# Choosing experts ahead of a pair's last scores, and an earlier running sum of chunk 1, in a fused gated-attention and mixture-of-experts kernel

## The chip, the cores and the metric

The kernel runs on one core of one Trainium2 chip. The metric is the device time of one execution in microseconds (us), from first to last instruction with what the device needs around them. A profiled execution also has a span: from the program's first instruction to its last.

The engines go by these names: PE is TensorE (matrix products; PEld its weight loads), DVE is VectorE, ACT is ScalarE, POOL is GpSimd, SP is SyncE, which here issues most DMAs. Each engine works through its own instructions in program order and waits on semaphores for the others.

## The reference

Two stages follow one another, in float32. The first is a gated linear recurrence over 4 sequences of 768 steps, with 8 heads of 48 numbers each:

```python
for t in range(S):
    state = alpha[:, :, t, :, None] * state + np.einsum('bhd,bhe->bhde', k[:, :, t], v[:, :, t])
    y[:, :, t] = np.einsum('bhd,bhde->bhe', q[:, :, t], state)
```

Its output becomes 3072 rows of 384 numbers. The second stage routes each row to one of 8 experts and runs that expert alone:

```python
logits = x @ w_gate
expert_idx = np.argmax(logits, axis=1)          # first of equals
h = np.maximum(x_sorted[lo:hi] @ w1[e], 0.0)    # 384 -> 1024, for each expert e
y_sorted[lo:hi] = h @ w2[e]                     # 1024 -> 384
out = gate_w[:, None] * y                       # gate_w: softmax weight of the chosen expert
```

## The kernel before, in words

**Chunks and pairs.** The 3072 rows are 24 chunks of 128 (NT = 24), six to a sequence (NB = 6). For a chunk s the kernel takes the logarithm of alpha (`logs`, L330, ACT), sums it along the chunk with a triangular matrix (`cums`, L341, PE, into the one PSUM tile `cum`), and raises it to exp in both signs (`icp` L344 and `cp` L345, ACT). `operands` (L364, L366, mostly POOL) multiplies k by icp and q by cp into `kqb`. `transposes` (L373, PE) turns both into the PSUM tiles `tp` (two buffers), and ACT and DVE copy them out to kT and qT (L376, L378). `scores` (L386, PE) multiplies them into the PSUM tiles sA and sB; DVE masks sA into dA (L390), ACT copies sB to dB (L392) and POOL masks it (L393). `weighs` (L430) multiplies the masked scores with v into y, `reads` (L418) adds what the state of the chunk before gives. `products` (L452) forms the state's increment in sA for odd chunks and in sB for even ones, so it has to wait until sA or sB was read. For odd chunks DVE adds the old state (accA, L458), and the next scores into sA wait for that; the last chunk of a sequence has no product. `state` (L467, L469, POOL) multiplies by the chunk's decay, which makes a round trip through memory (`decay_out` L350, `decay_in` L355).

**Rows and routing.** `results_to` (L442, DVE) takes y from PSUM. `rows` (L478, PE) turns it to rows and forms minus the logits; DVE sums these to `lgn` (L480). `keep_rows` (L485 ACT, L486 POOL) and `store_rows` (L491, SP) bring the rows to memory. `choose(g)` (L496 to L502, DVE) finds the expert of each row of a group g of chunks as a one-hot matrix `oh`; then POOL adds it to the running counts `ohs`, one addition per chunk (L504). Later `rank_products` (L509, L510, PE) and `slots_of` (L517 to L526, DVE) make a slot of each row, and `one_hots` (L579, L580, DVE), one chunk at a time from the list `hots`, prepares the products that list the tokens by slot (L541, L587). The groups are chunks 0-3, 4-7, 8-11, 12-15, 16-19, 20-21 and 22-23.

**Order.** The order is written out by hand, and the scheduler keeps it on every engine. After a start for chunks 0 to 6 (L629 to L698) comes a loop over pairs, s = 2, 4, ..., 20 (L700 to L779). A turn does reads, weighs and products of chunks s and s + 1, scores of s + 2, running sums and turnings of s + 3 and s + 4, rows of s and s + 1, scores of s + 3, then operands of s + 6, late constants on POOL (`late_consts`), and at its very end, where s + 1 closes a group, `choose` (in turn s = 20, called ORD, for the group 20-21). Loads stand in a list `to_load` and are issued by SP in places, with five buffers each for alpha, k and q. In the start, `keep_busy` (L616) puts products of zeros on PE where it would be idle.

**The experts.** The tail (L805 to L858) finishes chunks 22 and 23, and lists the tokens. Products of the first expert's first layer (`first_layer`, L789) are woven into the tail by `go_ahead(n)`, which issues n matmuls. Blocks of 128 rows are gathered from memory by POOL (L271), turned (`turn_block`, L964, PE), and go through both layers (L972, L988) expert after expert; the result goes out by an indirect DMA (L994). The first expert begins at L1044 with `go_ahead(9)`, ahead of the turning of block 2, the first of the second lot of gathered blocks.

Of the kernel before, what the change touches and what calls it, by code (L numbers as in the profile page):

```python
# [18 lines left out]
def kernel(  # L19
# [71 lines left out]
    ORD = NT - 4  # L91
# [197 lines left out]
    with tc.tile_pool(name="ld", bufs=6) as ld, \  # L289
# [21 lines left out]
        def some_loads(names):  # L311
            for n in names.split():
                load(n[0], int(n[1:]))
# [14 lines left out]
        def logs(s):  # L328
            st[s]["ln"] = work.tile([C, H, D], F32, name="ln")
            nc.scalar.activation(st[s]["ln"][:], st[s]["a"][:], AF.Ln)  # L330
# [7 lines left out]
        def cums(s):  # L338
            d = st[s]
            cum = rps.tile([C, Dm], F32, name="cum")  # L340
            nc.tensor.matmul(cum[:], lhsT=cmask[:], rhs=d["ln"][:], start=True, stop=True)  # L341
            d["icp"] = work.tile([C, Dm], F32, name="icp")
            d["cp"] = cpb[(s + 1) // 2 % len(cpb)][:, (s + 1) % 2, :, :D]
            nc.scalar.activation(d["icp"][:], cum[:], AF.Exp, scale=-1.0)  # L344
            nc.scalar.activation(d["cp"], heads(cum), AF.Exp)  # L345
# [22 lines left out]
        def transposes(s):  # L368
            d = st[s]
            for i, n in enumerate(("kT", "qT")):  # L370
                tp = ps.tile([C, NP, C], F32, name="tp", bufs=2)
                for p in range(NP):
                    nc.tensor.transpose(tp[:, p, :], pair(kqb[s % 4][:, i], p), ident[:])  # L373
                d[n] = work.tile([C, NP, C], F32, name=n, bufs=2 + i)
                if i:
                    nc.vector.tensor_copy(d[n][:], tp[:])  # L376
                else:
                    nc.scalar.copy(d[n][:], tp[:])  # L378
# [114 lines left out]
        def choose(g):  # L493

            t, n = slice(g[0], g[-1] + 1), len(g)
            nc.vector.tensor_reduce(lmin[:, t], lgn[:, t, :], axis=AX, op=ALU.min)  # L496
            sc = work.tile([C, n, E], F32, name="sc")
            nc.vector.tensor_tensor(sc[:], lgn[:, t, :], lmin[:, t].unsqueeze(2).to_broadcast([C, n, E]), op=ALU.is_le)
            nc.vector.tensor_tensor(sc[:], sc[:], first_w[:, None, :].to_broadcast([C, n, E]), op=ALU.mult)
            top = work.tile([C, n], F32, name="top")  # L500
            nc.vector.reduce_max(top[:], sc[:], axis=AX)
            nc.vector.tensor_tensor(oh[:, t, :], sc[:], top[:].unsqueeze(2).to_broadcast([C, n, E]), op=ALU.is_equal)  # L502
            for s in g:
                nc.gpsimd.tensor_add(ohs[:, s + 1, :], ohs[:, s, :], oh[:, s, :])  # L504

# [25 lines left out]
        def close_early(pos):  # L531

            cnt = work.tile([1, 1], F32, name="cnt")
            nc.vector.tensor_scalar(cnt[:], pos, scalar1=float(EC), scalar2=-1.0, op0=ALU.min, op1=ALU.mult)
            nc.vector.scalar_tensor_tensor(
                ohs[0:1, TE, 0:1], in0=cnt[:], scalar=float(EC), in1=ohs[0:1, TE, 0:1], op0=ALU.add, op1=ALU.add,
            )
# [69 lines left out]
        def do(f, i, *a):  # L607
            if 0 <= i < NT:
                f(i, *a)
# [16 lines left out]
        nc.scalar.preload_act_table_set("natural_log_exp_and_others")  # L626
        hots = []

        some_loads("a0 k0 q0 a1 k1 q1")  # L629
        first_consts()  # L630
        keep_busy(5)
        back_consts()
        for i in range(4):
            late_consts(i)
        logs(0)
        cums(0)
        keep_busy(3)
        operands(0, nc.vector, nc.vector)
        some_loads("a2 v0")
        decay_out(0, nc.scalar)  # L640
        logs(1)
        transposes(0)
        cums(1)
        operands(1)
        decay_in(0, nc.scalar)
        scores(0)
# [53 lines left out]
        for s in range(2, NT - 2, 2):  # L700
            more_loads(2)
            if s == 2:
                store_rows(0)
            do(decay_out, s + 4)
            more_loads(2)

            for _ in range(8 if s > NT - 8 else 0):
                next(parts, None)
            y = results_of(s)
            reads(s)  # L710
            reads(s + 1)

            weighs(s, 0)
            weighs(s, 1)
            products(s + 1)
            products(s + 2)
            weighs(s + 1, 0)
            results_to(s, y, 0)
            weighs(s + 1, 1)
            results_to(s, y, 1)  # L720
            state(s + 1)
            do(logs, s + 5)
            if hots:
                one_hots(hots.pop(0))
            scores(s + 2)
            do(logs, s + 6)
            do(cums, s + 5)
            ranks = y[0][:].rearrange("r i p t -> r (i p t)")
            ranked = [rank_products(g, ranks[:, : len(g) * E]) for g in groups_of if g[-1] == s - 1]
            counts = ranks[:, C : C + E]  # L730
            if s in (TE, ORD):

                nc.tensor.matmul(
                    counts, lhsT=ones_sq[:], rhs=ohs[:, s, :], start=True, stop=True, skip_group_check=True,
                )
            if s == ORD:
                early_slots(ranks[:, 2 * C : 2 * C + EB * NQ])
                fetch_lot(0)
            for r in ranked if s < ORD else ():
                slots_of(*r)  # L740
            transposes(s + 3)
            do(operands, s + 5)
            state(s + 2)
            rows(s)
            keep_rows(s)
            store_rows(s - 1)
            if s == ORD:
                for r in ranked:
                    slots_of(*r)
                key = standing(counts[0:1, :])  # L750
                one_hots(hots.pop(0))
                one_hots(hots.pop(0))
                route = rps.tile([C, Dm], F32, name="cum")
                tokens_of_slots(0, TE)
            do(cums, s + 6)
            do(transposes, s + 4)
            more_loads(5)
            do(decay_in, s + 4)
            rows(s + 1)
            keep_rows(s + 1)  # L760
            if s == TE:
                close_early(counts[0:1, 0:1])
            scores(s + 3)
            do(operands, s + 6)
            store_rows(s)
            if s == 2:

                nc.sync.dma_start(x_d[N // 2 : N // 2 + 1, :], zero_w[:])
            late_consts(s + 2)
            late_consts(s + 3)  # L770
            if s == ORD:
                choose(groups_of[-2])
            if hots:
                one_hots(hots.pop(0))
            for g in groups_of[:-2]:
                if g[-1] == s + 1:
                    choose(g)
            for _ in range(4 if s == NT - 8 else 0):
                next(parts, None)  # L779
        for _ in parts:  # L780
# [51 lines left out]
        keep_rows(s + 1)  # L832
        store_rows(s + 1)
        choose(groups_of[-1])
        tokens_of_slots(TE, NT - 4)
        go_ahead(3)

# [204 lines left out]

    for i in range(E):
        if i == 0:  # L1044
            go_ahead(9)
            for k in range(EB, needed[0][-1] + 1):
                turn_block(k)
                go_ahead(3)
            go_ahead(99)
            layer1(w_t[0][0], xT[0], h_t[0], EC, cols[0])  # L1050
        else:
            if i == E - 1:

                nc.gpsimd.drain()
            h_t[i] = (wk if i % 2 else early).tile([C, FB, CAP], F32, name="h_sb", bufs=1)
            if cols[i] < caps[i]:
                nc.gpsimd.memset(h_t[i][:, :, cols[i] : caps[i]], 0.0)
            layer1(w_t[i][0], xT[i], h_t[i], 0, cols[i])

        coming = list(needed[i + 1]) if i + 1 < E else []  # L1060
        for k in coming[:2]:
            turn_block(k)
        if i == 0:
            for n in (1, 2):
                weights1(n, True)
                weights2(n)
            gates_lot(0)
            gates_lot(1)
            for n in range(3, E):
                slots(n)  # L1070
            rows_out(o_idx[:], g_idx[:])
        if i + 3 < E:
            weights1(i + 3)
        for n, k in enumerate(ended[i]):
            if k not in gw:
                gates_lot([k in lot for lot in lots].index(True))
            results(k)
            if n == 0:
                for j in coming[2:]:
                    turn_block(j)  # L1080
                if i and i + 2 < E:

                    weights2(i + 2)
        if i in (0, 1, 3):
            fetch_lot((2, 3, None, 4)[i])
        if i == 0:
            nc.vector.tensor_copy(tot[:], route[0:1, NC : NC + E])
            extra_blocks()
# [48 lines left out]
```

## Time and profile before

| what | value |
|---|---|
| median of 10 runs | 431.08 us (429.81 to 432.19) |
| profiled execution, its own time | 431.05 us |
| its span | 429.3 us, granted TensorE clock 0.997 |
| busy in the span: PE / DVE / ACT / POOL | 419.6 / 142.4 / 108.1 / 141.4 us |
| moved by DMA | 59.43 MB |

By stage (view of windows: us of the window, then the busy time of each engine):

| stage | window | PE | DVE | ACT | POOL | DMA share |
|---|---|---|---|---|---|---|
| start, to the first scores | 0 to 10.20 | 8.72 | 6.71 | 3.93 | 4.33 | 0.85 |
| on to the middle of turn s = 4 | 10.20 to 49.06 | 37.77 | 19.07 | 21.49 | 25.56 | 0.94 |
| rest of the loop | 49.06 to 140.17 | 89.61 | 61.33 | 45.03 | 60.17 | 0.91 |
| tail | 140.17 to 158.85 | 18.02 | 12.67 | 5.47 | 6.96 | 0.30 |
| experts | 158.85 to 429.30 | 265.47 | 42.60 | 32.17 | 44.38 | 0.33 |

How to read the profile's lines. A timeline line has the start in us from the span's start, the duration in us, the engine, the line of the kernel, the operation, tile written <- tiles read, the shape, a count, and in brackets the engine's idle time before it with what ended it. A line of waits names who waited, for whom, the sum in us, how many times, and the longest. Matmuls overlap: the next group's first one usually starts a little before the last one of the group before has drained.

### The profile page before, as it was taken

Reading aid. Unit: us, or ns where it says so; the run is one execution under the profiler, and the core shown is the slowest. Engines: PE = TensorE matmul, PEld = TensorE weight load, DVE = VectorE, ACT = ScalarE, POOL = GpSimd, SP = SyncE. Lnnn points to the kernel's source line nnn. Section 1 sums busy time; section 2 is a strip of 40 time slices with the busy share of each in tenths; the row PEclk is TensorE's granted clock in tenths of the full one; section 3 lists DMA queues with packets and bytes.
Section 4 is the critical chain, followed back from the end, with each engine's and each line's share of the span. In section 5 each row is a group of like instructions: output and inputs, shape, how many; then the busy total and the mean of one; then the engine's idle time right before and its main releaser. Section 6 shows DMA issues by size and latency. Waiting matters only on the chain.

```text
span 429.3 us, 7702 instructions
## 1 busy us (share of the span) xinstructions
PE 419.6 (98%) x2990; PEld 284.7 (66%) x2990; DVE 142.4 (33%) x414; ACT 108.1 (25%) x230; POOL 141.4 (33%) x256
## 2 busy tenths in 40 slices
PE   8999999999999999999999999999999999999995
PEld 6888788888889888655555556655655455555452
DVE  6435657585858843721012101201201101111100
ACT  4465554555442321110111111011110111011011
POOL 4486677576665250160160120024010010011011
PEclk9999999999999999999999999999999999999998
DMA  8999999999977242995541710624530050000000
GB/s 166 170 167 205 198 202 188 202 194 196 185 205 206 95 104 75 397 398 177 192 113 51 274 37 14 259 83 116 214 117 18 2 183 20 0 33 20 1 33 30
DMA packets 132576, 59.43 MB, mean 138 GB/s; under 512 B 114614, under 2 KB 127452, under 8 KB 132538
## 3 DMA queue, kind: packets, MB, share of 16 engines
q1 hardware_dynamic: 127720, 48.96, 44.1%
q0 software_dynamic: 3328, 9.94, 7.1%
q8 instruction: 24, 0.39, 0.4%
q10 hardware_dynamic: 1490, 0.02, 0.2%
q14 instruction: 14, 0.11, 0.1%
HBM read 49.32 MB, written 9.98 MB: 138 GB/s over the span
## 4 chain that ended last, share of the span: by engine, by line
PE 60%; issue 28%; POOL 4%; DVE 4%; DMA 2%; ACT 1%; POOLq 0%; DVEq 0%; ACTq 0%; SPq 0%
PE zp L988 16%; PE hp L972 14%; PE sA L386 5%; PE xr L478 4%; PE tp L373 4%; PE y L430 4%; PE cum L341 3%; POOL out_dram L994 3%; PE y L418 2%; PE xr L616 2%; PE xtp L964 1%; POOL xg L271 1%; PE sB L452 1%; PE hp L789 1%; DMA a_sb<-in_alpha_dram 1%
## 5 line engine op out<-in xcount | busy, mean ns | idle before, releaser
L988 PE MATMUL zp<-w,h_sb 128*128 128x384 f32 (+2 forms) x560 | 137.1, 487 | 0.0
L972 PE MATMUL hp<-xT,w 128*128 128x416 f32 (+5 forms) x384 | 123.9, 483 | 0.0
L988 PEld LDWEIGHTS zp<-w,h_sb 128*128 128x128 f32 (+2 forms) x560 | 73.6, 163 | 56.3 <-issue 14.8
L972 PEld LDWEIGHTS hp<-xT,w 128*128 128x128 f32 x384 | 71.8, 190 | 50.7 <-issue 30.5
L994 POOL DMA_INDIRECT out_dram<-zo,o_idx x26 | 25.8, 992 | 213.3 <-ACT zo L993 208.4
L977 DVE TENSOR_SCALAR h_sb<-hp 128x416 f32<-128x416 f32 (+5 forms) x32 | 17.7, 554 | 148.1 <-PE hp L972 148.1
L993 ACT ACTIVATE zo<-zp,gw 128x384 f32<-128x384 f32 x26 | 15.1, 581 | 123.7 <-PE zp L988 119.1
L979 ACT ACTIVATE h_sb<-hp 128x416 f32<-128x416 f32 (+5 forms) x32 | 15.6, 488 | 106.1 <-PE hp L972 106.1
L386 PE MATMUL sA<-qT,kT 48*128 48x128 f32 x192 | 27.7, 285 | 1.4 <-DVE accA L458 1.1
L271 POOL DMA_INDIRECT xg<-x_rows,g_idx x26 | 25.1, 965 | 11.1 <-issue 6.4
L966 DVE COPY xT<-xtp 128x384 f32<-128x384 f32 (+3 forms) x29 | 13.1, 485 | 44.3 <-PE xtp L964 44.2
L386 PE MATMUL sB<-qT,kT 48*128 48x128 f32 x192 | 27.7, 285 | 0.0
L386 PEld LDWEIGHTS sA<-qT,kT 48*128 48x128 f32 x192 | 23.1, 187 | 6.0 <-issue 1.9
L364 POOL TENSOR_TENSOR kqb<-k_sb,icp 128x384 f32<-128x384 f32 x23 | 23.1, 1002 | 10.6 <-ACT icp L344 10.4
L373 PE MATMUL tp<-ident,kqb 128*128 128x128 f32 x192 | 25.6, 275 | 0.6 <-DVE qT L376 0.4
L430 PE MATMUL y<-dA,vb 128*64 128x128 f32 x192 | 25.9, 277 | 0.0
L373 PEld LDWEIGHTS tp<-ident,kqb 128*128 128x128 f32 x192 | 21.8, 141 | 6.0 <-issue 2.7
L430 PE MATMUL y<-dB,vb 128*64 128x128 f32 x192 | 25.4, 277 | 0.0
L478 PE MATMUL xr<-back,yT 128*128 128x104 f32 x192 | 25.2, 274 | 0.0
L478 PEld LDWEIGHTS xr<-back,yT 128*128 128x128 f32 x192 | 23.6, 192 | 1.0 <-ACT xs L485 0.4
L376 DVE COPY qT<-tp 128x512 f32<-128x512 f32 x24 | 16.6, 690 | 20.9 <-PE tp L373 20.7
L393 POOL TENSOR_SCALAR_AFFINE_SELECT dB<-dB 128x512 f32<-128x512 f32 x24 | 15.8, 657 | 22.6 <-ACT dB L392 22.6
(179 smaller groups left out, 447.8 us busy)
## 6 DMA issues: line engine op xcount, KB each, us to landing
w<-in_moe_w_dram SPq DMA_DIRECT2D x14, 1536.0 KB, 6.8
x_rows<-xs SPq DMA_DIRECT2D x24, 196.0 KB, 3.5
a_sb<-in_alpha_dram SPq DMA_DIRECT2D x24, 192.0 KB, 4.3
k_sb<-in_k_dram SPq DMA_DIRECT2D x24, 192.0 KB, 3.7
q_sb<-in_q_dram SPq DMA_DIRECT2D x24, 192.0 KB, 3.7
vb<-in_v_dram SPq DMA_DIRECT2D x24, 192.0 KB, 3.4
w<-in_moe_w_dram SPq DMA_DIRECT2D x12, 128.0 KB, 2.8
w<-in_moe_w_dram SPq DMA_DIRECT2D x8, 192.0 KB, 4.4
```

The lines of the kernel that those rows point to most:

```text
L271: nc.gpsimd.indirect_dma_start(out=xg[:, j, :], out_offset=None, in_=x_d[: N + 1 if n else TE * C + 1, :], in_offset=bass.IndirectOffsetOn ...
L364: k.tensor_tensor(kq[:, 0, :, :D], d["k"][:], heads(d["icp"]), op=ALU.mult)
L373: nc.tensor.transpose(tp[:, p, :], pair(kqb[s % 4][:, i], p), ident[:])
L376: nc.vector.tensor_copy(d[n][:], tp[:])
L386: nc.tensor.matmul(t[:, p, :], lhsT=d["kT"][r : r + D, p, :], rhs=d["qT"][r : r + D, p, :], start=True, stop=True,)
L393: nc.gpsimd.affine_select(d["dB"][:], d["dB"][:], compare_op=ALU.is_ge, fill=0.0, base=0, pattern=[[0, NP], [1, C]], channel_multiplier=-1,)
L430: nc.tensor.matmul(d["y"][h][at(p, a) : at(p, a) + DP, n, :], lhsT=d["v"][:, 2 * p + a, :], rhs=d["d" + "AB"[a]][:, p, :], start=(first an ...
L478: nc.tensor.matmul(xr[:, p, :], lhsT=d["yT"][:, p // (NP // 2), p % (NP // 2), :], rhs=back[:, p, :], start=True, stop=True)
L972: nc.tensor.matmul(hp[:, c0:c1], lhsT=w1[:, a, f * C : (f + 1) * C], rhs=xT[:, a, c0:c1], start=(a == 0), stop=(a == DB - 1),)
L977: nc.vector.tensor_relu(h[:, f, c0:c1], hp[:, c0:c1])
L988: nc.tensor.matmul(zp[i * wd : (i + 1) * wd, :], lhsT=h[:, f, c : c + wd], rhs=w2[:, f, :], start=(f == 0), stop=(f == FB - 1), skip_group ...
L994: ins = nc.gpsimd.indirect_dma_start(out=out[:, :], out_offset=bass.IndirectOffsetOnAxis(ap=idx, axis=0), in_=zo[:], in_offset=None, bound ...
```

## The change

Four things are changed; nothing is added to the work or taken from it.

1. In the loop, `choose` of a group stands right after the rows of its last chunk, ahead of the scores of chunk s + 3, in place of the turn's end. The running counts are split off as `sums` and stand after the operands of s + 6. A pair of one-hots that stood at a turn's end now stands ahead of those scores in turns that choose nothing, and stays at the end in turns that choose.
2. At the start, alpha of chunk 1 is loaded second. Its logarithm stands ahead of chunk 0's running sum, and its running sum ahead of the turning of chunk 0.
3. For chunk 0 alone, DVE copies kT and ACT copies qT; for all others it stays the other way round.
4. `go_ahead(9)` ahead of the turning of block 2 becomes `go_ahead(10)`.

```diff
-                if i:
+                if i == (s > 0):
                     nc.vector.tensor_copy(d[n][:], tp[:])
...
             nc.vector.tensor_tensor(oh[:, t, :], sc[:], top[:].unsqueeze(2).to_broadcast([C, n, E]), op=ALU.is_equal)
+
+        def sums(g):
             for s in g:
                 nc.gpsimd.tensor_add(ohs[:, s + 1, :], ohs[:, s, :], oh[:, s, :])
...
-        some_loads("a0 k0 q0 a1 k1 q1")
+        some_loads("a0 a1 k0 q0 k1 q1")
...
         logs(0)
+        logs(1)
         cums(0)
         keep_busy(3)
         operands(0, nc.vector, nc.vector)
         some_loads("a2 v0")
         decay_out(0, nc.scalar)
-        logs(1)
+        cums(1)
         transposes(0)
-        cums(1)
         operands(1)
...
+            chosen = [g for g in groups_of[:-2] if g[-1] == s + 1] + ([groups_of[-2]] if s == ORD else [])
+            for g in chosen:
+                choose(g)
+            if hots and not chosen:
+                one_hots(hots.pop(0))
             scores(s + 3)
             do(operands, s + 6)
+            for g in chosen:
+                sums(g)
             store_rows(s)
...
-            if s == ORD:
-                choose(groups_of[-2])
-            if hots:
+            if hots and chosen:
                 one_hots(hots.pop(0))
-            for g in groups_of[:-2]:
-                if g[-1] == s + 1:
-                    choose(g)
...
         choose(groups_of[-1])
+        sums(groups_of[-1])
...
-            go_ahead(9)
+            go_ahead(10)
```

## The prediction

> **What bounds the kernel now.** The stage table comes first: in every stretch TensorE is busy for 96% or more of the time, except in the first 10 us. TensorE goes through its instructions in program order, so a change gains only where TensorE waits, and whatever delays TensorE is lost unless a later wait takes it up. The second view is therefore the list of TensorE's own waits.
>
> ```profile
> engine line waited for: us in total, times, longest us
> PE sA L386 <- DVE accA L458: 1.1, 2, 0.7
> PE cum L341 <- ACT cpb L345: 0.8, 1, 0.8
> ...
> PE tp L373 <- DVE qT L376: 0.4, 1, 0.4
> PE xtp L964 <- DMA xg<-x_rows,g_idx: 0.2, 1, 0.2
> ```
>
> Here the reader is to see that two waits for accA and one for a qT copy, all on VectorE, make 1.5 us. TensorE's timeline places them: 0.40 at 67.69 and 0.74 at 89.78 (scores of chunks 8 and 14), 0.37 at 116.84 (turning of chunk 18). Each follows a loop turn that ends with the choice of four chunks (s = 6, 10, 14). A wait costs a little more than its idle time, since such groups otherwise start before the last one has drained: scores start 0.07 us before it (78.36 against 78.43), transposes 0.16. So 0.40 + 0.74 + 0.37 + 0.07 + 0.07 + 0.16 = **1.81 us**. After 158.85 no wait of TensorE's is listed at all: a shift there goes into the time undiminished.
>
> The third view is VectorE's timeline at the end of turn s = 10:
>
> ```profile
> 84.56 0.19 DVE L480 TENSOR_REDUCE lgn<-xr 128x8 f32<-128x32 f32 x1 [0.18 <-PE xr L478]
> 85.65 0.69 DVE L390 TENSOR_TENSOR dA<-sA,cmask 128x512 f32<-128x512 f32 x1 [0.89 <-PE sB L386]
> 86.26 0.28 DVE L579 TENSOR_SCALAR oh_r<-iota_r,rc 128x129 f16<-128x129 f32 x1
> 86.45 0.68 DVE L580 TENSOR_SCALAR oh_c<-iota_h,rc,tokv 128x129 f16<-128x129 f32 x1
> ...
> 87.25 0.81 DVE L498 TENSOR_TENSOR sc<-lgn,lmin 128x32 f32<-128x32 f32 x1
> 88.09 0.92 DVE L499 TENSOR_TENSOR sc<-sc,first_w 128x32 f32<-128x32 f32 x1
> ...
> 89.38 0.35 DVE L458 TENSOR_TENSOR accA<-sA,Ub 128x192 f32<-128x192 f32 x1
> ```
>
> The choice (L496 to L502) stands between oh_c and accA and takes from 87.05 to 89.46, while VectorE sat idle for 0.89 us before dA. Its two dear steps end with two GpSimd operations, as GpSimd's timeline shows:
>
> ```profile
> 87.01 1.00 POOL L364 TENSOR_TENSOR kqb<-k_sb,icp 128x384 f32<-128x384 f32 x1
> 87.97 1.00 POOL L366 TENSOR_TENSOR kqb<-q_sb,cpb 128x384 f32<-128x384 f32 x1
> ```
>
> In turn s = 18, where GpSimd is idle between 131.24 and 132.40, the same steps take a quarter of that, and the five together run from 131.24 to 132.31, 1.07 us:
>
> ```profile
> 131.45 0.19 DVE L498 TENSOR_TENSOR sc<-lgn,lmin 128x32 f32<-128x32 f32 x1
> 131.67 0.19 DVE L499 TENSOR_TENSOR sc<-sc,first_w 128x32 f32<-128x32 f32 x1
> ```
>
> **Part 1: the choice ahead of the scores.** It now waits only for lgn (end 84.75). GpSimd then has one 0.19 us copy (84.88) and nothing until 86.41, so the price is that of s = 18. First step 0.23 after lgn's start (as 147.32 to 147.55 in the tail), 84.79; last step ends 85.82. Behind it in VectorE's queue stand dA, one one-hot pair and accA. dA starts at 85.75 in place of 85.65 and ends 86.44; the product that overwrites sA comes at 87.07, so the 0.10 costs nothing. One-hots: 0.85 (86.26 to 87.13) if only oh_c meets GpSimd's mask, so to 87.3. accA waits for the product (87.07 + 0.62), then 0.35: 88.1. The scores want sA at 88.97. The wait of 0.81 goes, and 0.8 us of cover is left.
>
> The one-hots could meet more of GpSimd: if oh_r ends with the mask (87.05) and oh_c with the 1.00 product (88.01), accA ends at 88.5, still in time; only if oh_c also sat out the second one (88.97) would scores be 0.5 late. The skill's page "SBUF — State Buffer", section "SBUF: two separate sides", speaks against the place: it says that an exclusive lock goes to whichever of the two engines starts first, for its whole instruction, and oh_r is due within 0.1 us of the mask. It leaves open who wins here; by it the sum is the same unless GpSimd wins three times running.
>
> Turn 6 is alike: choice 62.60 to 63.63, dA ends 64.25, product at 65.31, accA by 66.4 where scores want it at 67.22; 0.47 goes. Turn 14 has no accA (chunk 17 ends a sequence): VectorE is some 0.7 us earlier through dA, rc and qT, which ends near 115.9 in place of 116.79, and the turning wants it at 116.32; 0.53 goes. Turns 2, 18 and 20 have no VectorE wait to lose; in 20 the two-chunk choice is followed by dA of chunk 23, ending about 142.05 where it is wanted at 142.2: nothing, with little cover.
>
> In the other turns a one-hot pair moves ahead of dA. Alone it takes 0.54 (142.18 to 142.72), less than the 0.89 idle: nothing. The four additions of a choice (1.03 on GpSimd) move ahead of constants in the same queue; the rank product that reads them comes 1 us later: nothing.
>
> What is late next? Loads: from chunk 13 on they land 1.5 us or more ahead of use (a 13: issued 58.42, 4.3 to land by the median, used 66.72; k 20: landed 98.56, used 109.56), so the gain isn't handed to the DMAs. Part 1: **-1.8**.
>
> **Part 2: the start.** SP now issues a1 second; k0 and q0 fall back by one load. First load landed at 3.67, sixth at 8.66: 1.0 each, so a1 at 4.7, k0 5.7, q0 6.7, wanted at 4.85, 7.55 and 8.02: nothing. ScalarE's second logarithm (0.52) fits between 4.85 and 7.03. But TensorE:
>
> ```profile
> 8.26 1.06 PE L373 MATMUL tp<-ident,kqb 128*128 128x128 f32 x8
> 9.16 0.81 PE L341 MATMUL cum<-ln,cmask 128*128 128x384 f32 x2
> 10.20 0.34 PE L386 MATMUL sA<-qT,kT 48*128 48x128 f32 x1 [0.23 <-DVE qT L376]
> ```
>
> Before, the running sum lies in the shadow of the two copies out of tp. Now it goes first (8.13 to 8.94), the eight transposes from 8.78 to 9.82; ScalarE, done with icp and cpb of chunk 1 at 9.84, copies qT (0.59) to 10.45 (VectorE, which now takes kT, is done with it by 10.2), and scores start at 10.57 in place of 10.20: **+0.37**. The earlier icp of chunk 1 brings kqb forward, but the turning of chunk 1 at 12.69 follows fillers (11.29 to 12.85), not kqb (12.55). So no gain is possible here; the ends are 0, and 0.8 if the whole sum (0.81) were unhidden. Does the 0.37 survive? TensorE waits 0.76 + 0.16 at 49.06 for cpb, behind a logarithm that waits for a10. If a10 landed when it did, the loss would vanish there. But SP has two real waits before, for cpb of chunk 2 (16.09) and 4 (25.40), and both follow TensorE, so its later issues shift too. I take +0.37.
>
> **Part 3: the tail.** One first-layer matmul more (go_ahead 10 in place of 9) stands before the turning that waits for the gather at 155.81. Six take 1.30, one 0.22; the wait is 0.24 + 0.16. Ends 0 and -0.40; **-0.22**.
>
> **Sum.** -1.81 + 0.37 - 0.22 = -1.66. The profiled execution took 431.05 (span 429.3), the median is 431.08; so **429.4**, span 427.7.
>
> **Rivals.**
> - The start is free, 0.16: a10 lands on its own schedule, the wait at 49.06 swallows 0.37. For: DMA share 0.94 up to there. Against: SP's two waits. 429.05.
> - A wait comes back, 0.12: oh_c meets two GpSimd products, or qT of the next turning is late; 0.8 at one place or split. 430.2.
> - The choice stays slow where it now stands, 0.10, 2.5 us as in turns 6 and 10. Then dA holds the sA product: turn 6 loses 0.5 for 0.47, turn 10 0.9 for 0.81, turn 18 0.4 anew, turn 20 0.3, turn 14 still gains 0.53: with start and tail +0.4, 431.5. Against: s = 18's row.
> - Slower, 0.10: the wider hole at 9.8 to 10.6 lets TensorE's clock fall. The first ten fillers take 4.64, the next six 1.46, so TensorE starts at half speed and needed some 5.6 us of work (1.25 to 6.8) to be quick; half speed for that long loses 2.8: 432.2. It decides if 0.8 us idle suffices. Against: the hole before 49.06 is 0.76 and the granted clock stays 1.00. The skill's page "TensorE: Matmul & The Clock Gate", section "What's actually happening", says that it falls after an idle window of about 3.4 us, which no run here shows; by it this price is nil and 429.4 stands.
>
> That the change doesn't do what it says is excluded by the instruction order: on VectorE L496 to L502 stand ahead of dA in all turns named.
>
> **Numbers.** 429.4 has 0.52. The range takes in the first three cases (0.80): below, 429.05 less the tail's other end (0.18) and some scatter of the median (runs 429.81 to 432.19); above, 430.2 and the same: 428.5 to 430.6. About 0.2% (0.86 us) is what a measurement here can tell from no change. Faster: 0.52 + 0.16 + 0.07 of the second rival = 0.75; same 0.05 + 0.08 = 0.13; slower 0.10 + 0.02 of the slow choice = 0.12.
>
> **To look for.** Right: no wait for accA L458 and no qT wait at the turning of chunk 18; L498 and L499 near 0.2 in all turns; first scores near 10.57; alpha wait near 49.4 with 0.7 or more idle; xtp's wait near nothing. Wrong: L498 at 0.8, a TensorE wait for dA L390, a granted clock under 1 after 10 us, or an alpha wait longer than 1 us.

## The result, and the profile after

The changed kernel takes 428.95 us (median of 12 runs, 427.42 to 429.64), the kernel before 431.07 (40 runs): a ratio of 0.9949, 95% interval 0.9939 to 0.9960, or 2.1 us faster. The prediction was 429.4 with a range of 428.5 to 430.6. The profiled execution took 428.3 with a span of 426.6, where before it took 431.05 and 429.3.

The list of TensorE's own waits in the changed kernel (line numbers after L502 are 2 to 6 higher than before):

```profile
PE xr L618 <- DVE still L118: 1.3, 1, 1.3
PE cum L341 <- ACT cpb L345: 1.2, 1, 1.2
PE sA L386 <- ACT qT L378: 0.7, 1, 0.7
PE hp L794 <- ACT h_sb L800: 0.4, 1, 0.4
PE tp L373 <- POOL kqb L366: 0.2, 1, 0.2
```

The two waits for accA, the one for qT at a turning and the gather's wait are gone. Two have grown: the first scores wait 0.7 for qT (0.23 before), and the alpha wait at the fifth turn (TensorE's wait for cpb at the running sum of chunk 10, where a late alpha tile holds ScalarE) is 1.2 (0.8 before). VectorE's timeline at the end of turn s = 10, and GpSimd's there:

```profile
83.72 0.19 DVE L496 TENSOR_REDUCE lmin<-lgn 128x4 f32<-128x32 f32 x1
83.94 0.19 DVE L498 TENSOR_TENSOR sc<-lgn,lmin 128x32 f32<-128x32 f32 x1
84.17 0.19 DVE L499 TENSOR_TENSOR sc<-sc,first_w 128x32 f32<-128x32 f32 x1
...
84.62 0.19 DVE L502 TENSOR_TENSOR oh<-sc,top 128x32 f16<-128x32 f32 x1
84.72 0.68 DVE L390 TENSOR_TENSOR dA<-sA,cmask 128x512 f32<-128x512 f32 x1
85.33 0.74 DVE L581 TENSOR_SCALAR oh_r<-iota_r,rc 128x129 f16<-128x129 f32 x1
85.98 1.05 DVE L582 TENSOR_SCALAR oh_c<-iota_h,rc,tokv 128x129 f16<-128x129 f32 x1
86.95 0.34 DVE L458 TENSOR_TENSOR accA<-sA,Ub 128x192 f32<-128x192 f32 x1
```

```profile
85.34 0.64 POOL L393 TENSOR_SCALAR_AFFINE_SELECT dB<-dB 128x512 f32<-128x512 f32 x1 [1.35 <-ACT dB L392]
85.95 1.00 POOL L364 TENSOR_TENSOR kqb<-k_sb,icp 128x384 f32<-128x384 f32 x1
```

The choice now takes 1.09 (83.72 to 84.81) in place of 2.41, and lies in VectorE's idle time. The two one-hot steps took its place beside GpSimd: each ends within 0.1 of one of GpSimd's operations (oh_r at 86.07, GpSimd's mask at 85.98; oh_c at 87.03, the product at 86.95). accA still ends at 87.29, 0.6 ahead of the scores at 87.91.

**Where the time went.** The same group of instructions is looked up in both traces, and the difference of its starts (after less before) is followed along the run:

| stretch | difference at its end | what happens in it |
|---|---|---|
| to the second fillers (6.82 before) | -1.05 | the first ten fillers take 4.03 instead of 4.64 and the first sum 0.81 instead of 1.30: TensorE's speed came up earlier |
| to the first scores (10.20) | -0.78 | the new order of sum, turning and copies: +0.27 |
| to the sum of chunk 10 (49.06) | -0.60 | 0.23 gained where the first ranks are formed (46.3), then the alpha wait is 1.17 instead of 0.76 |
| turn 6 to 8 | -1.07 | accA's wait gone: -0.47 |
| turn 10 to 12 | -1.87 | accA's wait gone: -0.81 |
| turn 14 to 16 | -2.68 | qT's wait gone: -0.80 |
| to the first expert (158.85) | -2.8 | the gather's wait gone |

The first row isn't the change's doing: up to 6.8 us TensorE runs the same instructions in both. All fourteen profiles, with those of the experiments below, confirm it: nine have the old order of the start, five the new one. From the start of the second fillers to the first scores the old order took 3.36 to 3.41, the new one 3.65 to 3.67 in four and 3.87 in one. But the second fillers themselves started anywhere from 5.72 to 6.96, in both orders. So the start has a part that differs from execution to execution by 1.2 us.

### The profile page after: what moved, and what is told of

Its sections match the earlier page's. It is cut to its first block, busy times and chain, and to the rows that moved or that the text cites. A ratio compares the mean times of both kernels' runs of the same rounds, so it can differ in the third digit from the quotient of the medians.

```text
span 426.6 us, 7699 instructions
## 1 busy us (share of the span) xinstructions
PE 417.7 (98%) x2990; PEld 283.9 (67%) x2990; DVE 138.2 (32%) x414; ACT 108.0 (25%) x230; POOL 141.2 (33%) x256
## 4 chain that ended last, share of the span: by engine, by line
PE 64%; issue 28%; POOL 4%; DMA 1%; ACT 1%; POOLq 0%; DVE 0%; SPq 0%; ACTq 0%
PE zp L994 16%; PE hp L978 14%; PE sA L386 6%; PE y L430 5%; PE xr L478 5%; PE tp L373 4%; PE cum L341 4%; POOL out_dram L1000 3%; PE y L418 3%; PE hp L794 2%; PE xr L618 2%; PE sB L452 1%; PE xtp L970 1%; POOL xg L271 1%; DMA a_sb<-in_alpha_dram 1%
## 5 line engine op out<-in xcount | busy, mean ns | idle before, releaser
L386 PEld LDWEIGHTS sB<-qT,kT 48*128 48x128 f32 x192 | 23.1, 187 | 0.0
```

Of the source, the lines that this page charges most:

```text
L386: nc.tensor.matmul(t[:, p, :], lhsT=d["kT"][r : r + D, p, :], rhs=d["qT"][r : r + D, p, :], start=True, stop=True,)
```

## The experiments

Each kernel was measured beside the kernel before, in several sets, and the medians of before differ a little between them (430.03 to 431.07), so ratios are compared. A ratio is formed over the runs; it isn't the quotient of the two medians and differs from it by up to 0.1%.

| kernel | median, us | before, us | ratio | 95% interval |
|---|---|---|---|---|
| the change | 428.95 | 431.07 | 0.9949 | 0.9939 to 0.9960 |
| e1: choice alone | 428.04 | 430.44 | 0.9947 | 0.9934 to 0.9960 |
| e2: start alone | 430.25 | 430.44 | 0.9998 | 0.9989 to 1.0007 |
| e4: choice and tail | 428.02 | 430.44 | 0.9950 | 0.9936 to 0.9965 |
| e5: old place, GpSimd behind | 431.42 | 430.44 | 1.0026 | 1.0015 to 1.0037 |
| e6: log behind | 431.32 | 430.06 | 1.0035 | 1.0022 to 1.0048 |
| e7: alpha sooner | 428.86 | 430.06 | 0.9972 | 0.9961 to 0.9983 |
| e8: alpha sooner, old start | 428.22 | 430.06 | 0.9951 | 0.9935 to 0.9966 |
| e9: e8 without second fillers | 427.25 | 430.06 | 0.9931 | 0.9917 to 0.9944 |
| e10: e8, ranks behind the rows | 427.76 | 430.03 | 0.9946 | 0.9932 to 0.9960 |
| e11: e10 without second fillers | 427.01 | 430.03 | 0.9933 | 0.9920 to 0.9947 |
| e12: e11, log behind | 426.73 | 430.03 | 0.9928 | 0.9915 to 0.9942 |
| e13: e12 with the changed start | 425.83 | 430.12 | 0.9909 | 0.9894 to 0.9923 |

### The parts: e1, e2 and e4

e1 has only the loop's part of the change; against the changed kernel, start and tail are as before (the start's other lines are left out here):

```diff
-        some_loads("a0 a1 k0 q0 k1 q1")
+        some_loads("a0 k0 q0 a1 k1 q1")
...
-            go_ahead(10)
+            go_ahead(9)
```

> The order of the loop's end is that of the changed kernel (choice and, in other turns, one-hots ahead of the scores, the four additions behind the operands); start and tail are as before. Theory (the three VectorE waits are the whole gain of this part): no wait of TensorE for accA or for a qT copy is left, 0.47 + 0.81 + 0.80 = 2.1 us as the two traces differ at turns 6, 10 and 14 (I had worked out 1.81), so 429.0 to 429.3; the alpha wait stays at 0.76 and the gather's wait at 0.24 or a little more. Rival (the start brought part of the gain: the first scores of the profiled execution came 0.78 earlier): 429.8 or more.

e2 has only the start's part (loads, logarithm, sum ahead of the turning, kT and qT exchanged), on the kernel before.

> Only the start is changed: a1 loaded second, its logarithm and running sum ahead of the turning of chunk 0, kT and qT copies swapped for chunk 0. Theory as on record: scores start 0.27 to 0.37 later against the end of the second fillers, and this stays or is taken up by the alpha wait: 431.1 to 431.5. Rival (the start is a gain; the 0.78 by which the first scores came early in the changed kernel's profile is its doing, not that of a TensorE clock that came up earlier in that execution): 430.3 to 430.6. By the theory the length of the first ten fillers differs from run to run of one and the same order, by the rival it doesn't.

e4 is e1 with the tail's part:

```diff
-            go_ahead(9)
+            go_ahead(10)
```

> The changed kernel with the start as before. Theory: the tail's additional matmul takes the gather's wait away, 0.2 to 0.4 beside the choice alone: 428.7 to 429.0, that is the same as or up to 0.3 less than the changed kernel's 428.95 (its start costs 0 to 0.3). Rival (the start gains): 429.3 to 429.7, slower than the changed kernel by what the start brings. Another rival (the tail's matmul doesn't count, since the gather lands with TensorE's earlier end): equal to the choice alone within 0.1.

Measured: 0.9947, 0.9998 and 0.9950. The choice alone is the whole gain (2.3 us by its ratio), the start is worth nothing that can be measured (-0.1 us, interval -0.5 to +0.3), and the tail's 0.2 lies under what e1 and e4 can tell apart, though its wait (0.22 in e1's profile) is not listed in e4's. e1's waits for accA and qT are gone as in the changed kernel. So the 0.78 by which the scores came early in the changed kernel's profile was no gain of the start.

What becomes of the start's 0.3 was looked for by setting these traces side by side. Each row has the sum of logits of chunk 3 (TensorE's place before the fifth turn), SP's issue of the load of alpha 10, ScalarE's logarithm of chunk 10, which waits for that tile, and the sum of logits of chunk 5, behind the alpha wait:

| profile | lgn of chunk 3 | alpha 10 issued | log of chunk 10 | lgn of chunk 5 | alpha wait listed |
|---|---|---|---|---|---|
| before | 39.83 | 43.49 | 47.73 | 51.76 | 0.8 |
| after | 39.07 | 42.87 | 47.13 | 51.16 | 1.2 |
| e1 | 38.72 | 42.29 | 46.59 | 50.62 | 1.0 |
| e4 | 39.37 | 43.08 | 47.49 | 51.53 | 1.2 |
| e2 | 40.26 | 42.11 | 46.85 | 51.17 | none |

Where there is a wait, lgn of chunk 5 comes 4.03 or 4.04 behind the logarithm, wherever TensorE stood. But in those four profiles alpha came in TensorE's order, 7.87 to 8.12 behind lgn of chunk 3: it was later by about as much as TensorE, as the prediction held. Only in e2 was TensorE the latest of the five and alpha the second earliest, 6.59 behind. The difference arises on SP: its issue that waits for cpb of chunk 4 stood at 25.84 in e2 and at 24.29 to 25.41 in the others, and alpha 10's followed 16.27 later in e2 and 18.00 to 18.23 later in the others. The start isn't what made SP quick there, for the changed kernel has e2's start and took 18.23, and e5 below, with the old start, took 16.74; what did isn't known. So that the alpha wait takes up what the start loses is seen in e2's profile alone, and isn't shown as a rule.

### The cause of the long choice: e5

The choice stays in its old place. Only GpSimd's operands are moved behind it.

```diff
             scores(s + 3)
-            do(operands, s + 6)
             store_rows(s)
...
                 if g[-1] == s + 1:
                     choose(g)
+            do(operands, s + 6)
```

> The kernel before with the choice left where it was, behind the scores, and only GpSimd's two operand products moved behind the choice and its four additions, so that GpSimd has nothing to do while VectorE chooses. Theory (the choice was dear because its two main steps ran beside GpSimd's products): L498 and L499 at 0.19 each, the choice 1.1 in place of 2.4 in turns 6 and 10, accA ends at about 88.5 in turn 10 where the scores want sA at 88.97, no wait for accA: 0.47 + 0.81 and most of 0.53 gained, 429.2 to 429.6, unless the operands, now some 2 us later on GpSimd, hold the next turning. Rival (the place in VectorE's queue is what counts, the choice is that long by itself): L498 and L499 stay at 0.8 to 0.9, the waits stay, 431.0 or more.

Measured 1.0026: slower than before, where the theory wanted 429.2 to 429.6. Its first half held. VectorE's timeline in turn 10 has L498 and L499 at 0.19 each, accA starts at 87.55, and neither accA wait is left; the alpha wait isn't listed here either. But another wait stands in the list:

```profile
PE tp L373 <- DVE lgn L480: 2.0, 3, 1.0
```

VectorE's timeline of the next turn shows where it comes from:

```profile
91.71 1.01 DVE L521 TENSOR_SCALAR rc_i<-slot_i 128x4 int32<-128x4 int32 x1
92.64 0.16 DVE L522 TENSOR_SCALAR rc_i<-slot_i 128x4 int32<-128x4 int32 x1
92.83 0.86 DVE L526 CAST rc<-rc_i 128x8 f32<-128x8 int32 x1
93.61 0.68 DVE L376 COPY qT<-tp 128x512 f32<-128x512 f32 x1
```

and GpSimd's beside it:

```profile
91.69 1.01 POOL L364 TENSOR_TENSOR kqb<-k_sb,icp 128x384 f32<-128x384 f32 x1
92.64 1.02 POOL L366 TENSOR_TENSOR kqb<-q_sb,cpb 128x384 f32<-128x384 f32 x1
```

GpSimd's products are only later. They now meet the five small steps that turn ranks into slots: two of them, on 8 or 4 numbers in a row, last about to the end of GpSimd's product beside them. The copy of qT behind them ends at 94.29, the lgn step behind it at 94.38, and TensorE's turning, idle for 0.99, starts at 94.43. (The profile names lgn as what it waited for; copy and lgn both stand behind the stretched steps.) So the cause of the long choice is shown, GpSimd's products; and they hinder other small VectorE steps that they meet.

### What else holds TensorE: e6 to e13

e6 is the changed kernel with ScalarE's order exchanged:

```diff
-            do(logs, s + 6)
             do(cums, s + 5)
+            do(logs, s + 6)
```

> The changed kernel with one exchange on ScalarE in every turn: the logarithm of chunk s + 6 is issued behind the two exponentials of chunk s + 5, so that a late alpha tile no longer holds the PSUM tile of the running sum. Theory (TensorE's place at the fifth turn is set by when alpha 10 lands, so that what the start wins or loses is taken up there; in the changed kernel's profile the logarithm runs from 47.13 to 47.65 and the sum of chunk 10 starts only at 48.46, 0.8 later, behind the two exponentials): the wait of 1.17 shrinks to about 0.4, ratio 0.9949 - 0.8/431 = 0.993, about 0.8 us under the changed kernel. Rival (the wait only moves to the exponentials of chunk 10 or a later alpha tile): the changed kernel's ratio, 0.995, within 0.1%.

Measured 1.0035: some 3.7 us slower than the changed kernel by the ratios, 2.2 by the profiled execution (430.48). The alpha wait is gone, and four waits for qT at turnings have come, 1.9 in all. The theory of where the wait would go failed: with the exponentials earlier, GpSimd's products come earlier, onto the five small steps, in four turns. At the fifth turn the wait for alpha had kept them apart: the first product starts at 46.34 in e6, and at 48.11, behind the late exponentials, in the changed kernel.

e7 removes the alpha wait by the load instead, e8 does so with the old start:

```diff
-                (...) if x == 7 else (("k", 0), ("v", -2), ("a", 1), ("q", 0))
+                (...) if x == 7 else (("k", 0), ("a", 1), ("v", -2), ("q", 0))
```

> The changed kernel with each pair's alpha tile loaded one place sooner, ahead of the v tile, from chunk 9 on. Theory (alpha 10's landing sets the fifth turn): it is issued at about 41 in place of 42.9 and lands before TensorE comes, no wait for cpb at the sum of chunk 10, 1.0 to 1.2 gained in place of the 0.8 of the other exchange: ratio 0.992 to 0.9925. Rival (v tiles, now one load later, become what TensorE waits for): a wait of TensorE for v at the products and no gain, 0.995 or more.

> The kernel with alpha one place sooner, and with the start of the kernel before. It tells whether the changed start costs anything once no late alpha tile takes it up. The prediction's term (the sum ahead of the turning makes the first scores 0.37 later): 0.3 to 0.4 less than the kernel with the changed start and alpha sooner, 0.1% of the time. Rival (the start is worth nothing either way, or the author's order is the better): equal within 0.05%, or more. The length of the first ten fillers is expected to vary between profiles by up to 1.1 us, whatever the order.

Measured 0.9972 and 0.9951, no gain in either. The logarithm of chunk 10 no longer waits for alpha in e7, and the wait only changes its name. VectorE in e7:

```profile
47.38 0.40 DVE L523 TENSOR_SCALAR rc_i<-slot_i 128x4 int32<-128x4 int32 x1
47.69 1.06 DVE L524 TENSOR_SCALAR rc_i<-slot_i 128x4 int32<-128x4 int32 x1
48.79 0.92 DVE L528 CAST rc<-rc_i 128x8 f32<-128x8 int32 x1
49.62 0.68 DVE L376 COPY qT<-tp 128x512 f32<-128x512 f32 x1
```

GpSimd's two products run from 47.73 to 49.67 there. TensorE behind it:

```profile
50.35 0.88 PE L373 MATMUL tp<-ident,kqb 128*128 128x128 f32 x6 [1.00 <-DVE qT L376]
```

With no alpha wait in either list, the changed start seems to cost: e7 against e8 is 0.2% (0.9 us by the ratios, 0.6 by the medians, 0.46 by the place of the first scores in the two traces, 10.83 and 10.37). The intervals overlap, so a cost isn't sure and its size is rough.

e9 is e8 without the six fillers behind the first scores:

```diff
         scores(0)
-        keep_busy(3)
```

> As the kernel with alpha sooner and the old start, and without the six fillers behind the first scores (1.46 us of TensorE; the operands of chunk 1 are ready at about 10.5, the turning starts at 11.6 to 12.8). Theory (the start counts undiminished once the alpha wait is gone, and TensorE's clock stays up over a hole of some 0.3 us): 0.8 to 1.3 less. Rival (a load or TensorE's clock takes it back): the next loads are late or TensorE runs slower, no gain, or a loss of up to 1.

Measured 0.9931 against 0.9951 for e8, some 0.9 us less, though again the intervals overlap. TensorE stays quick: each group of four transposes behind the new holes of 0.27 and 0.31 takes 0.66, as elsewhere. In this profile alpha 10 came late again (the logarithm at 47.12), and the alpha wait of 0.8 was back, while e8's wait of 1.0 for qT was not there; so the two profiles differ by more than the fillers. e10 and e11 below are a second pair that differs by the fillers alone (0.9946 and 0.9933).

e10 moves the five steps, e11 is e10 without the fillers, e12 adds the exchange of e6:

```diff
-            for r in ranked if s < ORD else ():
-                slots_of(*r)
             transposes(s + 3)
             ...
             store_rows(s - 1)
+            for r in ranked:
+                slots_of(*r)
```

> The kernel with alpha sooner and the old start (ratio 0.9951), with one more step moved: VectorE's five small steps that turn ranks into slots (own to rc) stand behind the turning of chunk s + 3 and the rows of chunk s, in every turn, and no longer ahead of the qT copy. Theory (with alpha sooner, GpSimd's products start 0.8 us earlier and two of those five steps, 0.4 and 0.17 us in the changed kernel, take 1.06 and 0.92 beside them, which delays qT and makes TensorE wait 1.0 at the turning of chunk 8): no such wait is left, 1.0 gained, ratio 0.993. Rival (the five steps wait for GpSimd in the new place as well and hold the next qT): 0.995 or more, and a wait of TensorE for a qT copy at a turning.

> As the run before it, without the six fillers behind the first scores. Theory: the 0.5 to 0.8 that the fillers cost beyond the operands' end at the start come through in part, since alpha 10 sets the fifth turn again (0.8 of wait in the run without fillers): ratio 0.992 to 0.993. Rival (alpha 10 takes it all up): equal to the run with fillers.

> As the run before it, and the logarithm of chunk s + 6 behind the exponentials of chunk s + 5. In the changed kernel alone this exchange cost 3 us, by the theory because GpSimd's products then came beside the five steps in four turns (4 waits for qT, 1.9 us by the profile, and no alpha wait in return). Theory: with the five steps out of the way it is harmless and takes up to 0.8 of alpha wait: ratio 0.991 to 0.992. Rival (the exchange itself is what costs, for instance by a later logarithm): 0.994 or more.

e10 measured 0.9946, hardly under e8's 0.9951 where 0.993 was expected. Its profile does what the theory says (no qT wait at a turning, no alpha wait in the list) and its profiled execution is 1.6 us shorter than e8's, of which 0.43 lies ahead of the first scores; but e8's profiled execution (429.17) is the longest of its runs. Why the medians differ by so little isn't settled. e11 and e12 measured 0.9933 and 0.9928: the exchange that cost the changed kernel 2 to 4 us costs nothing once the five steps stand elsewhere. This speaks for the collision, and against the exchange itself, as the cause in e6.

e13 is e12 with the changed start. 

> The kernel of the run before (alpha sooner, ranks behind the rows, the logarithm behind the exponentials, no fillers behind the first scores; ratio 0.9928), with the changed start in place of the old one. Theory (the changed start delays the first scores by 0.4 to 0.5, but brings GpSimd's operands of chunk 1 forward by more; the fillers hid that): in the changed kernel's profile those products end 0.1 before the first scores do, so TensorE's two waits for them (0.27 and 0.31) go; from the second fillers to the state product 5.7 in place of 6.4, 0.5 to 0.7 gained, ratio 0.991 to 0.9915. Rival (a later wait, for an alpha tile or a chain on ScalarE, takes it up): 0.9928 within 0.05%, and a new wait in the list. Another rival (the first scores' delay of 0.4 to 0.5 is all that counts, as with fillers): 0.9938.

Measured 0.9909, 4.3 us under before by the medians and 3.9 by the ratio. It is the fastest of all kernels here, and its interval lies clear of the changed kernel's. In e12 TensorE waited for the operands of chunk 1:

```profile
10.71 0.66 PE L373 MATMUL tp<-ident,kqb 128*128 128x128 f32 x4 [0.27 <-POOL kqb L364]
11.68 0.66 PE L373 MATMUL tp<-ident,kqb 128*128 128x128 f32 x4 [0.31 <-POOL kqb L366]
```

In e13 it doesn't, as its timeline and its whole list of waits show:

```profile
10.46 1.09 PE L373 MATMUL tp<-ident,kqb 128*128 128x128 f32 x8
```

```profile
PE xr L618 <- DVE still L118: 1.3, 1, 1.3
PE sA L386 <- ACT qT L378: 0.7, 1, 0.7
PE hp L791 <- ACT h_sb L797: 0.4, 1, 0.4
PE tp L373 <- POOL kqb L366: 0.2, 1, 0.2
```

From the second fillers to the third running sum it takes 6.37 (5.72 to 12.09) in place of 6.96 (5.91 to 12.87): 0.59 gained, as the theory had it, though the first scores come later. The two were measured on different chips and their intervals overlap, so 0.2% is the likely size, not a sure one.

## Why the prediction was right, and where it wasn't

**Part 1, -1.81: right, a little small.** The three waits are gone; they were worth 0.47, 0.81 and 0.80 (2.08), and e1 measured 2.3 with nothing else changed. The first two are as worked out. The third was put at 0.37 + 0.16 = 0.53: the mis-sized term of this sum. The wait for qT had cut a group of eight transposes in two, so the overlap of neighbouring groups was lost at the cut and behind it. Before and after:

```profile
115.88 0.60 PE L373 MATMUL tp<-ident,kqb 128*128 128x128 f32 x4
116.84 0.66 PE L373 MATMUL tp<-ident,kqb 128*128 128x128 f32 x4 [0.37 <-DVE qT L376]
```

```profile
114.00 1.04 PE L373 MATMUL tp<-ident,kqb 128*128 128x128 f32 x8
```

The eight took 1.57 before (115.88 to the next group at 117.45) and 0.88 after (114.00 to 114.88), which is 0.69, and another 0.11 went at the scores that follow.

**The price of the choice, 0.19 a step, and its cause: right.** In the changed kernel all choosing turns have L498 and L499 at 0.17 to 0.19, and e5 shows that GpSimd's products were the reason. **The cover of 0.8: too large.** The prediction counted one one-hot step beside GpSimd and named two as the bound. It was two, oh_r with the mask and oh_c with the first product, as the bound had it, and 0.6 of cover was left. oh_r and the mask started together, at 85.33 and 85.34, and it was oh_r that waited.

**Part 2, +0.37: the term that was wrong.** The order at the start does cost TensorE time there, 0.27 in the two profiles where 0.37 was worked out: the scores start 0.05 behind the end of the qT copy (9.37, 9.42), where 0.12 was reckoned. But "does it survive?" was answered wrongly, as far as the times go: e2 measured 0.9998, that is -0.5 to +0.3 us, which leaves out 0.37 though not 0.27, and the changed kernel and e4, which differ by the start alone, measured 0.9949 and 0.9950. The reason given was that SP's issues wait for TensorE, so that alpha 10 shifts with it. Alpha shifted so in four of the five profiles above and not in e2. Whether the 0.27 is taken up at the alpha wait, or is there and too small to see, stays open. The rival "the start is free", which had 0.16, fits the times, and its 429.05 is nearer to 428.95. That is partly luck: with the 2.08 of part 1 the prediction's sum gives 428.75 without a term for the start, and 429.02 with 0.27.

**Part 3, -0.22: right in the profile** (the wait went), too small for e1 and e4 to measure.

**Rivals.** Of the clock falling over the hole at the start there is no trace: the hole is 0.68 now, and the fillers behind the first scores take 1.56 as before. The granted clock that the prediction brought against this rival can't decide it: that view reads 1.00 for the first 6 us too, where a filler took 0.46 against 0.24 later; the durations can. e9, e11, e12 and e13 leave these fillers out and lose nothing. No choosing turn has a slow choice, and no late one-hot brought a wait back.

**What to look for.** The alpha wait was to be wrong if longer than 1 us. It was 1.17, and that pointed at the right term, but not at a cause: at lgn of chunk 4 TensorE was 1.01 earlier than before (47.33 against 48.34), and alpha 10 came 0.60 earlier, so most of the shift was shared. First scores at 9.42 and not near 10.57 are the quick first fillers of that execution.

## What to carry to other kernels

A wait that vanishes is worth its idle time and the overlap it cut, but only if no later wait, for a load say, takes it up; so follow a shift through the run to the next real wait, and compare several profiles before believing that a load moves with the engine, or that it doesn't: here alpha 10 did in four and didn't in a fifth. Before a small step is moved, look at what GpSimd does at the new place and at what takes the old one: e5, e6 and e7 each removed one wait and got another from the same collision. And try an edit that shows nothing again once its cover is gone: the changed start was worth nothing with the fillers, and by two profiles some 0.6 us without them.

## What the runs showed of the hardware

**Which VectorE steps GpSimd stretches.** Taken over five of the profiles (before, after, e5, e6, e12), median where no GpSimd operation of over 0.4 us overlaps the step, and where a product or an addition of two tiles does:

| step | reads | alone, us | beside it, us |
|---|---|---|---|
| sc (L498, L499) | two SBUF tiles | 0.19 | 0.81, 0.93 |
| oh_r, oh_c | SBUF tile and column | 0.28, 0.34 | 0.57, 0.66, up to 1.06 |
| rc cast | SBUF tile | 0.17 | 0.86 |
| rc_i (L521 to L524) | SBUF tile | 0.16 to 0.17 | 0.15 to 1.06 |
| lmin, slot_i (reductions) | SBUF tile | 0.17 to 0.19 | 0.17 to 0.19 |
| dA, qT, yT, accA, lgn, own | PSUM tile | 0.69, 0.69, 0.68, 0.36, 0.19, 0.18 | 0.69, 0.69, 0.69, 0.36, 0.19, 0.18 |

GpSimd's products into kqb take 0.98 to 1.03 in all five profiles, so at these meetings it is VectorE that pays. GpSimd's mask does the same: in e5's turn s = 2 it runs from 41.71 to 42.35, and L498, started at 41.83, takes 0.56. Steps that read PSUM and reductions don't pay. So, by these rows, dA can overlap GpSimd's mask or products at no cost, and the choice can't: its main steps read SBUF tiles alone. The Trainium skill's page "SBUF — State Buffer", section "SBUF: two separate sides", says that VectorE's operations with two SBUF inputs (against a GpSimd operation that reads SBUF) or in a two-port mode share one pair of ports with GpSimd under a lock, which goes to whichever starts first. The first half fits the rows with two tiles; whether the one-hots, the cast and rc_i run in such a mode no run here shows. The second half agrees with single cases, and no run tests it. In before, oh_r at 53.45 took its 0.28 though the mask began at 53.55. oh_c at 113.33 took 0.79 with the mask from 113.40, but the oh_r ahead of it ended only at 113.42: the record of a step begins a little before the step ahead has ended.

**The start of TensorE.** TensorE's instructions are the same in all fourteen profiles up to the second fillers, and these started at 5.72 to 6.96, a spread of more than half of the change's gain. The Trainium skill's page "TensorE: Matmul & The Clock Gate", section "What's actually happening", says that the activity window that releases the clock runs freely and isn't set by the kernel's start, so that the first fast matmul moves from run to run; the profiles here agree with it. One profile against one other can't tell a gain of some tenths at the start from this spread.
